# RWKV-7 then squared-Relu FFN: the state products by channel, products spread over array quarters, Relu squared in SBUF

## The chip, the cores and the metric

One core of a Trainium2 chip runs the whole program in one launch. The metric is the device time of that launch in microseconds. Thirteen runs of the kernel before gave a median of 1091.98 us (1089.86 to 1101.07).

The engines are TensorE (PE for its matmuls, PEld for its weight loads), VectorE (DVE), ScalarE (ACT), GpSimd (POOL) and SyncE (SP, which only issues transfers here). Each runs its own queue in program order and waits on semaphores for the others.

## The reference

Two blocks follow each other. The first is a recurrence over 768 tokens for 4 batches, 8 heads and 40 channels a head; the second a feed-forward network over all 3072 tokens.

```python
for t in range(S):                                   # B=4, H=8, S=768, D=40
    y[:, :, t] = einsum('bhd,bhde->bhe', rt, state)
    Sa = einsum('bhde,bhe->bhd', state, at)
    state_decay = state * wt[:, :, None, :] - einsum('bhd,bhe->bhde', Sa, bt)
    state = state_decay + einsum('bhd,bhe->bhde', vt, kt)
x = y.transpose(0, 2, 1, 3).reshape(B * S, H * D)    # 3072 x 320
h = maximum(x @ w_in, 0.0)                           # 320 x 2048
out = (h * h) @ w_out                                # 2048 x 320
```

Everything is float32.

## The kernel before

The sequence is cut into 6 chunks of 128 tokens; with 4 batches that makes 24 slots, numbered in the order chunk by chunk (`order`). Inside a chunk the recurrence is written as matrix products with a triangular inverse T, which is solved on POOL for several slots at once (`solve`), stored to DRAM and fetched back (`inverses`). Heads lie in pairs: head h is pair q = h//2, and half e = h%2 of the 128 partitions (40 of each 64 partitions are used, the rest are zero pads). The states are tiles of 128 x (4 pairs, 2 heads, 64), of which only the blocks of a head with itself are nonzero; the mask `same` keeps the others at zero.

Each slot consists of generators whose steps `weave` hands out over 12 common steps, in the order of the list `jobs`. What a generator emits in a step is appended to the queues of the engines in exactly that order; nothing is reordered afterwards.

- `chain(i)` is the serial part of slot i. It forms X = A'S + Av (tokens on partitions) from the masked product A, v, aT and the state; solves it in two halves of 64 tokens: T times the first half, N times that added to the second half, T times the second half; turns the result (`xnT`), grows the state by k'v + b'x, forms the masked product RX, and then the output y, which DVE scales into `tokens`. Between these products an ACT copy takes the result out of PSUM.
- `rest(i+1)` makes what the next slot needs: kvT (DVE, L503), the masked product A, the turned r and v (ACT copies L513 and L515), the state's decay (`f`, L521 to L524), the masked product RV, and k and b scaled.
- `prepare(i+8)` turns w, b, a, scans the decays, takes reciprocals (L357, L358, DVE), and forms N, which ACT copies out (L369) and SP stores for POOL's `solve`.
- `some(second, n)` runs n steps of the feed-forward network on groups of three finished slots: for each pair of the 16 blocks of 128 hidden channels, products of the tokens with `w_third` and `w_in`, Relu by ACT (L641), its product by DVE (L642); then the products with `w_out`.

PSUM is split into pools: `ps_w` with 4 banks (everything that `rest` and `prepare` turn or multiply, and RX), `ps_c` with 2 banks (the chain), `ps_f` with 2 banks (feed-forward). An allocation takes a bank whose last reader has been emitted, and its first product waits for that reader.

In slots 0 to 3 no feed-forward work runs; from slot 4 on ten feed-forward steps go into each slot; the last group of three slots is multiplied after slot 23, alone.

A float32 matmul shows as two records of weight load and matmul in the trace, a transposition as one.

Of the kernel before, what the change touches and what calls it, by code (L numbers as in the profile page):

```python
# [11 lines left out]
Alu = mybir.AluOpType  # L12
# [5 lines left out]
def kernel(  # L18
# [129 lines left out]
    def load(i, g=None):  # L148
        x_ = loaded[i] = {"k": fetch("k", k, i)}
        if g is not None:  # L150
# [14 lines left out]
    nc.gpsimd.memset(upper, 1.0)  # L165
    nc.gpsimd.affine_select(out=upper, in_=upper, compare_op=Alu.is_gt, fill=0.0, base=0,
                            pattern=[[1, 128]], channel_multiplier=-1)

    same = single("same", [128, NP, 2])
    nc.gpsimd.memset(same, 0.0)  # L170
    for e in range(2):
        nc.gpsimd.memset(same[e * DP:(e + 1) * DP, :, e:e + 1], 1.0)

    more_rings()
    x_ = loaded[0] = {nm: fetch(nm, src, 0) for nm, src in (("k", k), ("r", r))}
# [167 lines left out]
    def early(i, g=None):  # L343

        x_ = early_loaded.pop(i)
        dec = decays.next() if g is None else new("dec", [128, 3, NP, C + 2], 2)
        if g is not None:
            nc.vector.memset(dec[:, :A_, :, MID:MID + 1], 1.0)
        up, down, aT = (dec[:, n] for n in (UP, DOWN, A_))
        wT = turn(x_["w"])  # L350
        yield
        for q in range(NP):
            nc.vector.tensor_tensor_scan(up[:, q, MID + 1:C + 1], wT[:, q, MID:], ones, 1.0, Alu.mult, Alu.mult)  # L353
            nc.vector.tensor_tensor_scan(down[:, q, MID - 1::-1], wT[:, q, MID - 1::-1], ones, 1.0, Alu.mult, Alu.mult)
        yield
        bT_, aT_ = turn(x_["b"]), turn(x_["a"])
        nc.vector.reciprocal(down[:, :, MID + 1:C + 1], up[:, :, MID + 1:C + 1])  # L357
        nc.vector.reciprocal(up[:, :, :MID], down[:, :, :MID])  # L358
        yield
        bT = turned("bT", 1)  # L360
        nc.vector.tensor_tensor(bT, bT_, down[:, :, 1:C + 1], Alu.mult)
        nc.vector.tensor_tensor(aT[:, :, :C], aT_, up[:, :, :C], Alu.mult)  # L362
        if g is None:
            store(kept_e[i], dec)
        yield
        bb, c = order[i]
        t_ = new("N", [128, H, C], 1)
        for e, p_ in enumerate(products(bT, aT[:, :, :C])):
            nc.scalar.copy(t_[:, e * NP:(e + 1) * NP], p_)  # L369
        joins = lambda half: t_[half * HC:half * HC + Q, :, half * HC + Q:(half + 1) * HC]  # L370
        for half in range(2):
            for n in range(2):
                at = half * HC + n * Q
                if i < SMALL:
                    kept, to = kept_q[i, :, half, n], at + Q
                else:
                    u = unit_of[i]
                    kept, to = kept_d[u][i - units[u][0], :, half], (half + 1) * HC
                    kept = kept[:, n * Q * HC:n * Q * HC + Q * (to - at)].rearrange("h (s t) -> h s t", s=Q)
                store(kept.rearrange("h s t -> s h t"), t_[at:at + Q, :, at:to], 1, nc.scalar if g is not None and n else nc.sync)  # L380
            if i < SMALL and g is None:
                store(kept_m[i][half], joins(half), 1)
        if g is None:
            store(kept_n[i], t_[:HC, :, HC:], 1)
        else:
            g["dec"], g["N"] = dec, new("N21", [HC, H, HC], 2)
            nc.scalar.copy(g["N"], t_[:HC, :, HC:])
            g["joins"] = spare("joins", i)
            for half in range(2):
                nc.scalar.copy(g["joins"][half * HC:half * HC + Q], joins(half))  # L390
        yield
# [99 lines left out]
    def rest(i, g):  # L491
        bb, c = order[i]
        x_ = loaded.pop(i)
        dec = g["dec"]
        up, down, aT = dec[:, UP], dec[:, DOWN], dec[:, A_, :, :C]
        ends = new("ends", [128, NP], 2)
        g["up"], g["aT"] = up, aT
        yield

        kT, rT = turned("kvT", 1), turned("rT", 2)  # L500
        kT_ = turn(x_["k"])
        yield
        nc.vector.tensor_tensor(kT, kT_, down[:, :, 1:C + 1], Alu.mult)  # L503
        nc.vector.tensor_copy(ends, down[:, :, 0])
        joining = inverses(i, g) if i else iter(())
        if soon(i):
            next(joining, None)
        yield
        g["A"] = masked("A", 2, kT, aT)
        yield  # L510
        while "v" not in x_:
            line.pop(0)[1]()
        nc.scalar.copy(rT, turn(x_["r"]))  # L513
        vT = turned("kvT", 1)
        nc.scalar.copy(vT, turn(x_["v"]))  # L515
        g["rT"] = rT
        yield
        if c > 0:
            st = states.tiles[bb]
            f_ = new("f", [128, NP, 2], 1)  # L520
            nc.vector.tensor_tensor(f_[:, :, 0], ended[bb], ends, Alu.mult)  # L521
            nc.vector.tensor_copy(f_[:, :, 1], f_[:, :, 0])
            nc.vector.tensor_tensor(f_, f_, same, Alu.mult)
            nc.vector.tensor_tensor(st[:, :, :, :D], st[:, :, :, :D],  # L524
                                    f_.unsqueeze(3).to_broadcast([128, NP, 2, D]), Alu.mult)
        g["RV"] = masked("RV", 4, vT, rT)
        if i and unit_of[i] < FINE:
            next(joining)
        yield
        p_ = psum(ps_w)  # L530
        for q in range(NP):
            nc.tensor.transpose(p_[:, q * 128:(q + 1) * 128], down[:, q, 1:C + 1], ident)  # L532
        inv = p_.rearrange("t (h d) -> t h d", h=H)[:, :, :D]
        yield
        for nm in ("k", "b"):
            nc.vector.tensor_tensor(x_[nm][:, :, :D], inv, x_[nm][:, :, :D], Alu.mult)
            g[nm] = x_[nm]
        g["v"] = x_["v"]
        if c > 0:
            p_ = psum(ps_c)  # L540
            for q in range(NP):
                nc.tensor.transpose(p_[:, q * 128:(q + 1) * 128], st[:, q].rearrange("p e d -> p (e d)"), ident)  # L542
            sd = g["sd"] = new("sd", [128, NP, 2, DP], 2)
            nc.scalar.copy(sd.rearrange("p q e d -> p q (e d)"), quads(p_))
        yield
        yield from joining
        yield


    ended, tokens = {}, {}  # L550
    order_of = lambda h: (h % 2) * NP + h // 2

    def chain(i, g):
        bb, c = order[i]
# [1 line left out]
        aT, rT, k_, b_, v_ = (g[x] for x in ("aT", "rT", "k", "b", "v"))  # L556
        sd = g.get("sd")
        first, second_ = slice(0, HC), slice(HC, C)
        x_ = by_head(psum(ps_c))
        for h in range(H):  # L560
            mm(x_[:, h], g["A"][h % 2][:, h // 2], v_[:, h, :D], h == 0)
        if c > 0:
            for q in range(NP):
                mm(x_[:, 2 * q:2 * q + 2], aT[:, q], st[:, q, :, :D], False)
        xr = new("xr", [128, H, D], 1)
        nc.scalar.copy(xr[first], x_[first])
        yield
        T, N = g["T"], g["N"]
        xn = minus_x.next()
        xs = by_head(psum(ps_c))  # L570
        for h in range(H):
            mm(xs[first, h], T[first, order_of(h)], xr[first, h], h == 0)
        nc.scalar.copy(xn[first, :, :D], xs[first])
        yield
        for h in range(H):
            mm(x_[second_, h], N[:, order_of(h)], xn[first, h, :D], False)
        nc.scalar.copy(xr[second_], x_[second_])  # L577
        yield
        for h in range(H):
            mm(xs[second_, h], T[second_, order_of(h)], xr[second_, h], h == 0)  # L580
        nc.scalar.copy(xn[second_, :, :D], xs[second_])
        yield
        p_ = psum(ps_c)
        for q in range(NP):
# [2 lines left out]
        nc.scalar.copy(xT, quads(p_))  # L587
        yield
        if c < NCH - 1:
            grown = psum(ps_c)[:, :NP * 2 * D].rearrange("p (q e d) -> p q e d", q=NP, e=2)  # L590
            for q in range(NP):
                mm(grown[:, q], pair(k_, q), v_[:, 2 * q:2 * q + 2, :D], q == 0)
            for q in range(NP):
                mm(grown[:, q], pair(b_, q), xn[:, 2 * q:2 * q + 2, :D], False)
            nc.vector.tensor_tensor(st[:, :, :, :D], grown, st[:, :, :, :D], Alu.add)
            ended[bb] = new(f"end{bb}", [128, NP], 1)
            nc.vector.tensor_copy(ended[bb], g["up"][:, :, C])
            yield
# [27 lines left out]
    def ffn():  # L626
        for gi in range(len(order) // GB):
# [4 lines left out]
            for f in range(0, NF, 2):  # L632
# [4 lines left out]
                for e, p_ in enumerate(ps):  # L637
# [1 line left out]
                        mm(p_, w_in[:, j, (f + e) * 128:(f + e + 1) * 128], t_[:, j, :], False)  # L639
                    h_ = hidden[:, f + e]  # L640
                    nc.scalar.activation(h_, p_, Act.Relu)  # L641
                    nc.vector.tensor_tensor(h_, p_, h_, Alu.mult)  # L642
                    hid.append(h_)
                    yield True
            while left():
# [118 lines left out]
    for i in range(len(order)):  # L764
# [1 line left out]
        n, begin = share.get(i, (10, 0))  # L766
        tc.no_sync_barrier()
        g = ready.pop(i)
        jobs = [(chain(i, g), 9, 0, TOTAL) if i else (first_slot, 8, 0, TOTAL)]
        if i + 1 < len(order):  # L770
            if i:
                ready[i + 1] = {}
                load(i + 1, ready[i + 1])
            jobs.append((rest(i + 1, ready[i + 1]), 9, 2, TOTAL))
        made = ahead.get(i, ())
        for j, m_ in enumerate(made):
            jobs.append((prepare(m_), 5, j * 5, TOTAL - 5 * (len(made) - 1 - j)))
        done.update(made)
        jobs.append((some(second, n), n, begin, TOTAL))
        if i in pieces_in:  # L780
            m_, end = pieces_in[i]
            jobs.append((some(rounded, 2 * m_), 2 * m_, 0, end))
# [38 lines left out]
```

## Time and profile before

| what | value |
|---|---|
| median of 13 runs | 1091.98 us |
| the profiled execution | 1096.39 us, of which the span from first to last instruction 1094.7 us |
| PE busy | 994.3 us (91%), 7248 matmul records |
| DVE, ACT, POOL busy | 471.7 us (43%), 235.6 us (22%), 651.4 us (60%) |
| mean granted clock of TensorE | 0.906 |
| chain that ended last | PE 73%, DVE 8%, DMA 7%, POOL 7% |

In the page, a group is one line of code, engine, operation and shape: its busy time, the mean of one instruction, and the idle time before it with what ended it. A matmul's duration contains its latency, and matmuls overlap; what a group of matmuls costs PE is read from the timeline, as the start of the group after it minus its own start.

### The profile page before, as it was taken

The page shows a single profiled execution, that of the slowest core. Times are in us where ns is not written, and L with a number is a line of the kernel's source. Part 1 is how long each engine was busy: PE and PEld are TensorE (multiplying, and loading weights), DVE is VectorE, ACT ScalarE, POOL GpSimd, SP SyncE. Part 2 cuts the span into 40 slices and gives each one's busy share as a digit, 9 for nine tenths or more (in the row PEclk, how much of TensorE's full clock was granted, in tenths as well). Part 3 has the DMA queues.
Part 4 walks back from the last instruction along what each step waited for, and adds up shares of the span by engine and source line. Part 5 has one row for each costly group of instructions (what it writes and reads, how often), then busy time and mean ns, then how long its engine had stood idle before and what let it go on. Part 6 is the DMA issues. An engine that isn't in the chain of part 4 may idle for free.

```text
span 1094.7 us, 18413 instructions
## 1 busy us (share of the span) xinstructions
PE 994.3 (91%) x7248; PEld 745.9 (68%) x7248; DVE 471.7 (43%) x940; ACT 235.6 (22%) x483; POOL 651.4 (60%) x1127
## 2 busy tenths in 40 slices
PE   6386667889999999999999999999999999999798
PEld 5275556777677767777677667766786777667556
DVE  6458676687463264333462453252323322331030
ACT  2133232342221113113211222113112211230020
POOL 5787636884885999923999903999858820000000
PEclk8666655569999999999999999999999999999899
DMA  9879977749729615348616528424244331330000
GB/s 119 150 145 184 170 208 149 153 121 175 141 53 214 125 48 96 97 116 157 127 47 114 119 83 156 114 54 80 54 115 92 68 85 31 75 62 7 22 1 18
DMA packets 261350, 113.42 MB, mean 104 GB/s; under 512 B 243792, under 2 KB 249424, under 8 KB 259600
## 3 DMA queue, kind: packets, MB, share of 16 engines
q1 hardware_dynamic: 256928, 93.24, 43.1%
q0 software_dynamic: 3248, 18.88, 7.2%
q8 instruction: 57, 0.93, 0.4%
q10 hardware_dynamic: 1088, 0.13, 0.1%
q14 instruction: 29, 0.24, 0.1%
HBM read 75.77 MB, written 34.48 MB: 101 GB/s over the span
## 4 chain that ended last, share of the span: by engine, by line
PE 73%; DVE 8%; DMA 7%; POOL 7%; issue 3%; SPq 2%; ACT 1%; DVEq 0%; POOLq 0%; ACTq 0%
PE ps_f L87 34%; PE ps_c L87 19%; PE ps_w L87 13%; PE ps_w L316 4%; POOL half_t L434 3%; POOL half_p L432 3%; DMA blocks<-kept_t 1%; DVE decay L357 1%; SPq L108 1%; DMA half_n<-kept_d 1%; PE ps_w L532 1%; DVE decay L358 1%; PE ps_c L542 1%; DMA kept_e<-decay 1%; PE ps_c L585 1%
## 5 line engine op out<-in xcount | busy, mean ns | idle before, releaser
L432 POOL TENSOR_TENSOR half_p<-half_n,half_t 128x70 f32<-128x70 f32 (+52 forms) x502 | 288.9, 576 | 101.5 <-DMA half_n<-kept_d 52.2
L434 POOL TENSOR_TENSOR half_t<-half_t,half_p 128x70 f32<-128x70 f32 (+52 forms) x502 | 314.8, 627 | 39.3
L87 PE MATMUL ps_f<-w_out,hid 128*128 128x320 f32 x672 | 197.7, 438 | 0.0
L87 PE MATMUL ps_f<-tokens,w_in 128*128 128x384 f32 x448 | 171.8, 508 | 0.0
L642 DVE TENSOR_TENSOR hid<-ps_f,hid 128x384 f32<-128x384 f32 x112 | 61.7, 551 | 229.9 <-ACT hid L641 229.2
L87 PEld LDWEIGHTS ps_f<-w_out,hid 128*128 128x128 f32 x672 | 121.4, 190 | 43.7 <-issue 0.2
L87 PEld LDWEIGHTS ps_f<-tokens,w_in 128*128 128x128 f32 x448 | 77.2, 192 | 63.3 <-issue 32.2
L641 ACT ACTIVATE hid<-ps_f 128x384 f32<-128x384 f32 x112 | 54.9, 490 | 216.0 <-PE ps_f L87 216.0
L87 PEld LDWEIGHTS ps_c<-xr,T 64*64 64x64 f32 x768 | 54.4, 149 | 26.2 <-issue 21.7
L87 PE MATMUL ps_c<-xr,T 64*64 64x40 f32 x768 | 60.3, 240 | 4.4 <-ACT xr L577 1.8
L87 PE MATMUL ps_f<-tokens,w_third 64*128 64x384 f32 x224 | 62.4, 540 | 0.8 <-DVE hid L642 0.8
L87 PEld LDWEIGHTS ps_c<-in_v,A 128*128 128x128 f32 x384 | 53.2, 217 | 4.1
L87 PE MATMUL ps_c<-in_v,A 128*128 128x40 f32 x384 | 52.6, 302 | 0.0
L332 DVE TENSOR_TENSOR A<-ps_w,upper 128x512 f32<-128x512 f32 x48 | 30.9, 685 | 47.2 <-PE ps_w L87 47.2
L409 POOL DMA_DIRECT2D half_n<-kept_d x18 | 8.9, 501 | 68.4 <-DMA kept_d<-N 68.1
L332 DVE TENSOR_TENSOR RX<-ps_w,upper 128x512 f32<-128x512 f32 x48 | 30.8, 684 | 39.8 <-PE ps_w L87 39.7
L353 DVE TENSOR_TENSOR_SCAN decay<-ps_w,ones 128x64 f32<-128x64 f32 x88 | 23.5, 267 | 51.2 <-PE ps_w L316 51.2
L503 DVE TENSOR_TENSOR kvT<-ps_w,dec 128x512 f32<-128x512 f32 x24 | 16.4, 682 | 63.7 <-PE ps_w L316 36.7
L87 PE MATMUL ps_w<-decay,bT 40*128 40x128 f32 x352 | 28.3, 306 | 16.2 <-DVE decay L362 12.3
L87 PE MATMUL ps_w<-rT,xnT 40*128 40x128 f32 x384 | 33.0, 298 | 10.0 <-DVE RV L332 8.6
L87 PEld LDWEIGHTS ps_w<-rT,xnT 40*128 40x128 f32 x384 | 27.5, 199 | 20.5 <-DVE RV L332 14.5
L614 DVE TENSOR_TENSOR tokens<-ps_c,dec 128x512 f32<-128x512 f32 x24 | 16.5, 688 | 57.1 <-PE ps_c L87 57.1
(138 smaller groups left out, 1456.7 us busy)
## 6 DMA issues: line engine op xcount, KB each, us to landing
kept_e<-decay SPq DMA_DIRECT2D x22, 780.0 KB
dec<-kept_e SPq DMA_DIRECT2D x22, 780.0 KB
hid<-in_moe_w_out_dram SPq DMA_DIRECT2D x16, 320.0 KB
half_n<-kept_d POOLq DMA_DIRECT2D x12, 384.0 KB, 10.0
half_n<-kept_d POOLq DMA_DIRECT2D x6, 768.0 KB, 10.4
in_w<-in_w_dram SPq DMA_DIRECT2D x24, 160.0 KB
in_ab<-in_b_dram SPq DMA_DIRECT2D x24, 160.0 KB
in_ab<-in_a_dram SPq DMA_DIRECT2D x24, 160.0 KB
```

The costliest lines, as they stand in the source:

```text
L87: nc.tensor.matmul(o, l_, r_, start=start, stop=True, skip_group_check=True)
L108: later(lambda: queue.dma_start(out=out_, in_=in_), steps)
L316: nc.tensor.transpose(p_[:, q * 128:(q + 1) * 128], pair(x_, q), ident)
L332: nc.vector.tensor_tensor(t_, p_, over4(upper), Alu.mult)
L353: nc.vector.tensor_tensor_scan(up[:, q, MID + 1:C + 1], wT[:, q, MID:], ones, 1.0, Alu.mult, Alu.mult)
L357: nc.vector.reciprocal(down[:, :, MID + 1:C + 1], up[:, :, MID + 1:C + 1])
L432: nc.gpsimd.tensor_tensor(p_, part[:, at:at + m_].unsqueeze(1).to_broadcast([128, n, m_]), t3[:, :n, s:s + 1].to_broadcast([128, n, m_]), ...
L434: nc.gpsimd.tensor_tensor(t3[:, :n, s + 1:], t3[:, :n, s + 1:], p_, Alu.subtract)
L503: nc.vector.tensor_tensor(kT, kT_, down[:, :, 1:C + 1], Alu.mult)
L614: nc.vector.tensor_tensor(t_, y_, g["up"][:, :, :C], Alu.mult)
L641: nc.scalar.activation(h_, p_, Act.Relu)
L642: nc.vector.tensor_tensor(h_, p_, h_, Alu.mult)
```

## The change

1. In `chain`, X is formed transposed: for each head, v (128 tokens x 64) and the head's state block (64 x 64) are the stationary operands, and A and aT move past them (128 columns). Each head's result lies in its own 64 partitions, channels on partitions. ACT copies it out, four transpositions bring it back to tokens on partitions, and one ACT copy takes it into `xr`. This adds one step with a wait of PE for ACT.
2. For odd heads the two halves of 64 tokens are swapped: in X by reading A and aT in the order second half, first half; in N by where `prepare` copies N out (one ACT copy of 128x512 becomes three of 64x4x64). So in `times_t` even and odd heads use the array quarters (0,0) and (64,64) in turn, and N's products write output columns 64 to 127 and 0 to 63 in turn. Every copy out of these products becomes two of half the size.
3. The state's growth is made head by head (8 products of 64x40 from each of k and b, written to the head's 64 partitions) in place of pair by pair (4 of 128x80), and added and decayed by two DVE operations each of 64 partitions. The mask `same` and two small DVE operations on `f` go.
4. In the feed-forward network DVE squares the Relu from SBUF (`h_ * h_`) in place of multiplying it with the PSUM bank.
5. `jobs`: the feed-forward steps stand right behind the chain's, then `prepare`, then `rest`; before, it was chain, `rest`, `prepare`, feed-forward. The chain's steps are handed out as 11 (10 in slot 0) where they were 9 (8).

```diff
@@ early
-        for e, p_ in enumerate(products(bT, aT[:, :, :C])):
-            nc.scalar.copy(t_[:, e * NP:(e + 1) * NP], p_)
+        even, odd = products(bT, aT[:, :, :C])
+        nc.scalar.copy(t_[:, :NP], even)
+        for half in range(2):
+            own_, other = (slice(n * HC, (n + 1) * HC) for n in (half, 1 - half))
+            nc.scalar.copy(t_[own_, NP:, own_], odd[other, :, other])
+        nc.scalar.copy(t_[:HC, NP:, HC:], odd[:HC, :, HC:])
@@ rest
-            nc.vector.tensor_copy(f_[:, :, 1], f_[:, :, 0])
-            nc.vector.tensor_tensor(f_, f_, same, Alu.mult)
-            nc.vector.tensor_tensor(st[:, :, :, :D], st[:, :, :, :D],
-                                    f_.unsqueeze(3).to_broadcast([128, NP, 2, D]), Alu.mult)
+            for e in range(2):
+                own_ = st[e * DP:(e + 1) * DP, :, e, :D]
+                nc.vector.tensor_tensor(own_, own_, f_[e * DP:(e + 1) * DP].unsqueeze(2).to_broadcast([DP, NP, D]), Alu.mult)
@@ chain
-        for h in range(H):
-            mm(x_[:, h], g["A"][h % 2][:, h // 2], v_[:, h, :D], h == 0)
+        xw = quads(psum(ps_c))
+        for h, q, e, rows in heads:
+            mm(swap(xw[rows, q], 0), v_[:, h, :], swap(g["A"][e][:, q], e), h < 2)
         if c > 0:
-            for q in range(NP):
-                mm(x_[:, 2 * q:2 * q + 2], aT[:, q], st[:, q, :, :D], False)
+            for h, q, e, rows in heads:
+                mm(swap(xw[rows, q], 0), st[rows, q, e, :], swap(aT[rows, q], e), False)
+        xc = turned("xnT", 1)
+        nc.scalar.copy(xc, xw)
+        yield
+        p_ = psum(ps_c)
+        for q in range(NP):
+            nc.tensor.matmul(p_[:, q * 128:(q + 1) * 128], xc[:, q], ident, start=q == 0, stop=True, is_transpose=True, ...)
+        x_ = p_.rearrange("t (h d) -> t h d", h=H)[:, :, :D]
         xr = new("xr", [128, H, D], 1)
-        nc.scalar.copy(xr[first], x_[first])
+        nc.scalar.copy(xr, x_)
         yield
...
+        def times_t(half):
+            xs = psum(ps_c)[:, :NP * D].rearrange("p (q d) -> p q d", q=NP)
+            for h, q, e, _ in heads:
+                rows = halves[half ^ e]
+                mm(xs[rows, q], T[rows, order_of(h)], xr[rows, h], h < 2)
+            nc.scalar.copy(xn[halves[half], ::2, :D], xs[halves[half]])
+            nc.scalar.copy(xn[halves[half], 1::2, :D], xs[halves[1 - half]])
...
+        for h, q, e, _ in heads:
+            mm(x_[halves[1 - e], h], N[:, order_of(h)], xn[first, h, :D], False)
+        nc.scalar.copy(xr[second_, ::2], x_[second_, ::2])
+        nc.scalar.copy(xr[first, 1::2], x_[first, 1::2])
...
-            for q in range(NP):
-                mm(grown[:, q], pair(k_, q), v_[:, 2 * q:2 * q + 2, :D], q == 0)
-            for q in range(NP):
-                mm(grown[:, q], pair(b_, q), xn[:, 2 * q:2 * q + 2, :D], False)
-            nc.vector.tensor_tensor(st[:, :, :, :D], grown, st[:, :, :, :D], Alu.add)
+            for l_, r_ in ((k_, v_), (b_, xn)):
+                for h, q, e, rows in heads:
+                    mm(grown[rows, q], l_[:, h, :], r_[:, h, :D], l_ is k_ and h < 2)
+            for e in range(2):
+                rows = slice(e * DP, (e + 1) * DP)
+                nc.vector.tensor_tensor(st[rows, :, e, :D], grown[rows], st[rows, :, e, :D], Alu.add)
@@ ffn
-                    nc.vector.tensor_tensor(h_, p_, h_, Alu.mult)
+                    nc.vector.tensor_tensor(h_, h_, h_, Alu.mult)
@@ the slots
-        jobs = [(chain(i, g), 9, 0, TOTAL) if i else (first_slot, 8, 0, TOTAL)]
+        jobs = [(chain(i, g), 11, 0, TOTAL) if i else (first_slot, 10, 0, TOTAL)]
+        jobs.append((some(second, n), n, begin, TOTAL))
+        (prepare for each of ahead[i])
         if i + 1 < len(order):
             ...
             jobs.append((rest(i + 1, ready[i + 1]), 9, 2, TOTAL))
-        (prepare for each of ahead[i])
-        jobs.append((some(second, n), n, begin, TOTAL))
```

## The prediction

> **What bounds the kernel now.** I read the page's slices first, then busy time by slot, then the timeline of one slot for PE, then the waits.
>
> ```profile
> PE   6386667889999999999999999999999999999798
> PEclk8666655569999999999999999999999999999899
> ...
> 497.54:537.46 39.92, 39.24 (x289) 27.43 (x288) 19.64 (x39) 9.90 (x20) 24.20 (x38) 1.00 0.74 156
> ```
>
> From about 230 us on PE never rests, at full clock from about 312 us. The windows row is slot 10 (from its Av to the next one): of 39.92 us PE is busy 39.24, DVE 19.64, ACT 9.90. So from slot 4 to the end a microsecond taken from PE's stream is a microsecond of time, and a new wait of PE costs in full. Before 230 us PE, DVE, POOL and transfers wait for each other. The timeline of PE says what each group costs: start of the next minus own start.
>
> ```profile
> 490.24 1.09 PE L87 MATMUL ps_c<-RV,in_k 128*64 128x128 f32 x16
> 491.16 1.04 PE L87 MATMUL ps_c<-RX,in_b 128*64 128x128 f32 x16
> ...
> 497.54 1.87 PE L87 MATMUL ps_c<-in_v,A 128*128 128x40 f32 x16
> 499.24 1.10 PE L87 MATMUL ps_c<-state,dec 128*128 128x80 f32 x8
> 500.27 0.92 PE L87 MATMUL ps_f<-tokens,w_third 64*128 64x384 f32 x4
> ...
> 502.60 1.12 PE L87 MATMUL ps_c<-xr,T 64*64 64x40 f32 x16
> 503.66 0.66 PE L316 MATMUL ps_w<-ident,in_w 128*128 128x128 f32 x4
> ...
> 514.49 0.60 PE L585 MATMUL ps_c<-ident,minus_x 128*128 128x128 f32 x4
> 515.02 1.16 PE L87 MATMUL ps_w<-dec,kvT 40*128 40x128 f32 x16
> 516.11 1.12 PE L87 MATMUL ps_c<-in_v,in_k 128*128 128x80 f32 x8
> 517.07 1.06 PE L87 MATMUL ps_c<-minus_x,in_b 128*128 128x80 f32 x8
> 517.96 0.60 PE L316 MATMUL ps_w<-ident,in_r 128*128 128x128 f32 x4
> ```
>
> Av costs 1.70 us, 106 ns a record, though only 40 columns move: loading 128 weight columns sets it. The form 128*64 with 128 columns moving, even and odd heads on the two column halves, costs 0.92 us for 16 (57 ns).
>
> **Part 1, X by channel.** Av takes just that form: 1.70 to 0.92, -0.78. A'S: 8 records in 1.03 become 16 of 64*64 with 128 columns, on opposite quarters; the A product (40*128, alternating row halves) costs 1.09 for 16, so 1.0 is taken: 0. One more change of form between the two: +0.10. Four transpositions as at 514.49: +0.53. Sum -0.15. Their waits for ACT (0.59 for 128x512, 0.42 for `xr`) lie behind a feed-forward step of 1.4 to 2.3 us.
>
> **Part 2, quarters.** T costs 1.06 for 16, 66 ns, again loading weights. With neighbours on opposite quarters two can load at once; what then? The smallest records of the trace:
>
> ```profile
> 194.75 1.09 PE L87 MATMUL ps_w<-blocks,hid 32*32 32x32 f32 x32
> 195.77 2.61 PE L87 MATMUL ps_c<-in_v,A 128*128 128x40 f32 x15
> ```
>
> 1.02 us for 32, 32 ns each. So 16 x 32 plus 0.10 for the change of form: 0.61, -0.45 each; T twice and N (1.06 too): -1.35. Bounds: 0 if they don't overlap, -0.53 at half.
>
> Two rules of the Trainium skill speak against this. "TensorE: Matmul & The Clock Gate", Part 2, puts PE's sequencer at about 62 ns per matmul where hardware decoding is off; then T at 66 is at the floor already and part 2 brings nothing. The 32 ns above decides against it. "TensorEngine Tiling", Restrictions and Gotchas (PSUM Pressure), says that different row tiles can't access one PSUM bank at once. T's quarters and A'S are different row tiles in one bank; the trace's row-tiled products (A, RV) write two banks, so no full group tests it. By the rule T stays at 1.06 twice and A'S goes to 16 x 112 ns = 1.8 us (112 as the 128-column records of the state's product run now): +1.7 a slot against my sum. In the 32x32 group, halves on different row tiles share a bank, and no gap shows inside it; their partitions differ, as here. I take the overlap.
>
> **Part 3, growth.** 0.96 + 0.89 = 1.85 becomes 32 records of 128*64 with 40 columns. RV's 57 ns is for 128 columns moving; if loads on the two column halves overlap, 32 x 32 + 0.10 = 1.1, -0.75; if not, 32 x 58 = 1.86 and nothing. I take the first: in the RV group the loads start in pairs 7 ns apart. DVE: two operations more and two fewer (0.17 to 0.57 each), hidden.
>
> PE in a slot: -0.15 - 1.35 - 0.75 = -2.25 with growth (15 slots, 5 to 19), -1.5 without (20 to 23), about -2.0 in slot 4: -33.8 - 6.0 - 2.0 = **-42 us**.
>
> **Part 5, the order: what now waits.** In step 5 of a slot the feed-forward step stands before kvT on DVE, and A comes one step later with only the turn of xn between. In the slot above:
>
> ```profile
> 514.69 0.49 ACT L641 ACTIVATE hid<-ps_f 128x384 f32<-128x384 f32 x1 [2.22 <-PE ps_f L87]
> 515.21 0.56 DVE L642 TENSOR_TENSOR hid<-ps_f,hid 128x384 f32<-128x384 f32 x1 [2.34 <-ACT hid L641]
> ...
> 518.60 0.59 ACT L513 COPY rT<-ps_w 128x512 f32<-128x512 f32 x1 [2.83 <-PE ps_w L316]
> 519.08 0.59 ACT L515 COPY kvT<-ps_w 128x512 f32<-128x512 f32 x1
> ```
>
> kvT (0.68) would run after 515.77, end at 516.4, and A start at 516.45 in place of 515.02: 1.43 us. It happens where step 5 is a hidden block (slots 7, 8, 10, 13, 15, 16, 18, 19, 21, 22); where it is a `w_out` step DVE has nothing before kvT. With part 4's wait below 1.6: **+16**. Then r and v are turned directly before RX, which takes their two banks: v's copy ends at 519.67, and RX, free to start at 518.83 by PE, starts at 519.7 less two records: 0.85 in slots 4 to 19, **+13.6**. RV then waits for RX's masks behind the reciprocals (3.4 us on DVE): the wait for RX covers nearly all, **+2**.
>
> What goes: the waits before the turn of the decays and before RX.
>
> ```profile
> PE ps_w L87 <- DVE RV L332: 8.6, 5, 3.1
> PE ps_w L532 <- DVE RX L332: 8.3, 12, 1.2
> ```
>
> RX, y and a feed-forward step now lie between: **-15** of these 16.9. Net of the order: +17.
>
> **Part 4, the square from SBUF.** The bank is free 0.56 us sooner, but PE waited for `hid` under 1 us in all (L642 delays PE by 0.8): 0. What it costs:
>
> ```profile
> L523 DVE TENSOR_TENSOR f<-f,same x20: 166/168/1099, 222.9 to 985.8; 128x8 f32<-128x8 f32 x20
> ```
>
> An operation with two SBUF inputs takes 168 ns, or up to 1099 where POOL is at work (570 at 523.30); L642, reading PSUM, never leaves 487 to 559. So the square will wait up to a POOL instruction, some 0.3 us in the mean, which counts only where PE waits for DVE (in the 1.6). POOL waits too: some 17 squares of 0.3 us per solve of 131 us, +5; T of slots 10, 14 and 18 lands some 20 us before its use, the slots' gain takes 6: hidden.
>
> ACT gains about 1.7 us a slot (copies halved, X's copy, N's three) on 9.90 of 39.92: hidden. In slots 0 to 4 nothing covers the new step (PE waits 0.6 to 0.9 for each copy, N's copies 0.6 later for POOL), while PE's saving counts double at the half clock. Between +4 and -8; I take -2. SP's and POOL's transfers keep their order within their slots; `same`'s memsets (under 1 us) are in this.
>
> **Sum:** 1096.39 - 42 + 17 - 2 = 1069.4 on the profiled execution, which lay 4.4 above the median: 1065 for the median.
>
> **Rivals.**
> A, the forecast: 1065, own range 1050 to 1078 (waits for A and RX half or double by 7, early slots -8 to +4). Chance 0.60.
> B, column halves don't overlap their loads: N and growth bring nothing, 15 x 1.2 + 4 x 0.45 + 1 = +21: 1086. For it: no group in the trace is bound by loads on alternating columns. 0.14.
> C, the bank rule holds: T and A'S lose 1.7 a slot in 19 slots, +32: 1097, slower. It decides from 1.4 a slot on, where PE's remaining saving no longer pays for the +17. Against it: the 32x32 group, and that the quarters' partitions differ. 0.13.
> D, the new waits are mostly covered (DVE's kvT or ACT's copies come early): +17 becomes 0: 1048. Against it: the queues are in order. 0.08.
> E, POOL and DVE hold each other up so that T arrives late in slots 10, 14 and 18, some 4 us each, and the waits double: about 1098. 0.05.
> That the products don't alternate as the change says: in the program's order they take quarters (0,0) and (64,64) in turn, so no.
>
> **Numbers.** About 0.3% (3.3 us) is what a measurement can tell. Faster: A, D and most of B: 0.77. Same: part of B and C: 0.06. Slower: C and E: 0.17. The range leaves out E's upper half, part of C and D's lower part: 1046 to 1096.
>
> **What would show it.** T's group near 0.6 us, N's the same, growth near 1.1, Av near 0.95; PE idle before A released by DVE kvT in hidden-block slots, before RX by ACT kvT in all of 4 to 19, and none before the turn of the decays; a slot of some 38.5 us for 39.9. Wrong if T stays at 1.06 or A'S at 1.8 (C), growth at 1.85 (B), or if slots 0 to 4 move by over 8 us.

## The result and the profile after

The changed kernel takes 1060.04 us (median of 11 runs, 1055.22 to 1068.03), the kernel before 1092.84 us (median of 48): ratio 0.9705, interval 0.9685 to 0.9725. That is 32.8 us less. The prediction was 1065, 27 us less on its own profiled execution; the profiled execution of the changed kernel took 1062.1 us, 34.3 less than the one it was predicted from.

First the page of the changed kernel: the slices of PE and its clock, and the row of the square.

```profile
PE   6375668769999999999999999999999999999898
...
PEclk8666556578889999999999999998999999999899
...
L664 DVE TENSOR_TENSOR hid<-hid 128x384 f32<-128x384 f32 x128 | 95.1, 743 | 244.2 <-ACT hid L663 243.9
```

PE is full from the same slice on as before. The clock row has an 8 in the middle where before had only 9s. The square from SBUF takes 743 ns in the mean; the product that read PSUM took 551 before.

Then slot 10, which is the slot that the prediction showed. The windows row gives span, PE, PEld, DVE, ACT, POOL, then the granted clock and DMA:

```profile
481.42:520.61 39.19, 37.61 (x318) 25.27 (x316) 20.36 (x40) 11.40 (x26) 21.28 (x34) 0.96 0.66 131
```

39.19 us for 39.92 is a poor slot: PE is idle for 1.6 us of it and the clock stands at 0.96 in place of 1.00. Both show in PE's timeline of the slot. What a group costs is the next start minus its own:

```profile
481.42 1.09 PE L87 MATMUL ps_c<-A,in_v 128*64 128x128 f32 x16
482.45 1.10 PE L87 MATMUL ps_c<-dec,state 64*64 64x128 f32 x16
483.48 0.92 PE L87 MATMUL ps_f<-tokens,w_third 64*128 64x384 f32 x4
...
485.71 0.60 PE L577 MATMUL ps_c<-ident,xnT 128*128 128x128 f32 x4
486.15 1.46 PE L87 MATMUL ps_f<-tokens,w_in 128*128 128x384 f32 x4
...
487.97 0.66 PE L87 MATMUL ps_c<-xr,T 64*64 64x40 f32 x16
488.56 0.92 PE L87 MATMUL ps_f<-tokens,w_third 64*128 64x384 f32 x4
...
490.90 0.66 PE L87 MATMUL ps_c<-minus_x,N 64*64 64x40 f32 x16
491.49 1.56 PE L87 MATMUL ps_f<-tokens,w_in 128*128 128x384 f32 x4
...
496.25 0.60 PE L606 MATMUL ps_c<-ident,minus_x 128*128 128x128 f32 x4
498.18 1.16 PE L87 MATMUL ps_w<-dec,kvT 40*128 40x128 f32 x16 [1.34 <-DVE kvT L503]
499.27 0.67 PE L87 MATMUL ps_c<-in_v,in_k 128*64 128x40 f32 x16
499.76 0.77 PE L87 MATMUL ps_c<-minus_x,in_b 128*64 128x40 f32 x16
500.46 2.93 PE L87 MATMUL ps_f<-tokens,w_in 128*128 128x384 f32 x4
...
504.68 0.60 PE L311 MATMUL ps_w<-ident,in_v 128*128 128x128 f32 x4
505.51 1.53 PE L87 MATMUL ps_w<-rT,xnT 40*128 40x128 f32 x15 [0.24 <-ACT rT L513]
```

Av costs 1.03 us for 1.70, A'S 1.03, the turn of X 0.44, T and N 0.59 each for 1.05. Growth is 1.19 here (499.27 to 500.46) and 1.06 in 13 of 20 slots, for 1.85. Before A stands the new wait: 496.25 to 498.18, of which 1.34 us is named as idle. DVE shows why, the square first and kvT behind it:

```profile
496.97 0.56 DVE L664 TENSOR_TENSOR hid<-hid 128x384 f32<-128x384 f32 x1 [1.34 <-ACT hid L663]
497.44 0.68 DVE L503 TENSOR_TENSOR kvT<-ps_w,dec 128x512 f32<-128x512 f32 x1
```

Just behind that wait the feed-forward group at 500.46 costs 2.73 us where 1.4 is usual. The windows of 2 us there say that this is the clock (the trace's own clock records put it at 0.50 from 500.13 to 503.54 us):

```profile
500.00:502.00 2.00, 2.00 (x17) 1.32 (x14) 1.40 (x5) 0.00 (x0) 1.41 (x5) 0.53 0.94 113
502.00:504.00 2.00, 2.00 (x9) 1.29 (x8) 0.04 (x1) 0.49 (x1) 1.69 (x5) 0.61 0.96 151
```

To see where the whole gain lies I added up PE's timelines of both traces over slots 5 to 19, where the stream is dense. A group is charged from its start to the next start; where the last record of a group and the first of the next start over 0.7 us apart, that counts as a wait, less 0.2. The 15 slots took 608.7 us before and 587.3 after.

| term, slots 5 to 19, us | predicted | measured |
|---|---|---|
| Av, A'S, turn of X | -2.3 | -9.4 + 1.4 + 6.6 = -1.5 |
| T and N | -20.3 | -13.8 - 6.9 = -20.7 |
| growth | -11.3 | -9.4 |
| wait before A | +13 (8 slots by 1.6) | +13.5 |
| wait for the decays at the same place, slot 5 | - | +2.1 |
| wait for ACT before RX | +12.8 | +5.2 |
| waits of before that go | -15 | -11.5 |
| products with `w_third` | 0 | -6.8 |
| two short waits of before (T, `w_in`) | - | -1.9 |
| RV behind RX's masks | +2 | in the rest |
| rest (5.1 of it half clock) | - | +9.6 |
| sum | -21 | -21.4 |

Slots 0 to 4 gave 6.4 us and slots 20 to 23 with the end 6.9; the prediction had 4 and about 3 there.

### The profile page after: what moved, and what is told of

Read it like the earlier page. It is cut to its first block, busy times and chain, and to the rows that moved or that the text cites. A ratio compares the mean times of both kernels' runs of the same rounds, so it can differ in the third digit from the quotient of the medians.

```text
span 1060.4 us, 19794 instructions
## 1 busy us (share of the span) xinstructions
PE 946.7 (89%) x7824; PEld 685.6 (65%) x7824; DVE 501.6 (47%) x940; ACT 272.0 (26%) x627; POOL 667.2 (63%) x1124
## 4 chain that ended last, share of the span: by engine, by line
PE 77%; DVE 6%; DMA 6%; issue 3%; ACT 3%; POOL 3%; SPq 1%; DVEq 0%; POOLq 0%; ACTq 0%
PE ps_f L87 38%; PE ps_c L87 17%; PE ps_w L87 16%; PE ps_w L311 4%; POOL half_t L434 1%; POOL half_p L432 1%; DMA in_w<-in_w_dram 1%; DMA dec<-kept_e 1%; SPq L108 1%; DMA in_k<-in_k_dram 1%; DMA kept_e<-decay 1%; DVE decay L352 1%; PE ps_c L577 1%; DMA w_out<-in_moe_w_in_dram 1%; PE ps_w L531 1%
## 5 line engine op out<-in xcount | busy, mean ns | idle before, releaser
L434 POOL TENSOR_TENSOR half_t<-half_t,half_p 128x70 f32<-128x70 f32 (+52 forms) x502 | 323.3, 644 | 39.4
L664 DVE TENSOR_TENSOR hid<-hid 128x384 f32<-128x384 f32 x128 | 95.1, 743 | 244.2 <-ACT hid L663 243.9
L87 PE MATMUL ps_f<-tokens,w_in 128*128 128x384 f32 x448 | 179.9, 526 | 0.0
L87 PEld LDWEIGHTS ps_w<-decay,bT 40*128 40x128 f32 x352 | 25.1, 213 | 37.3 <-DVE decay L357 21.4
L87 PE MATMUL ps_w<-dec,kvT 40*128 40x128 f32 x384 | 33.0, 318 | 16.4 <-DVE kvT L503 16.4
L327 DVE TENSOR_TENSOR RX<-ps_w,upper 128x512 f32<-128x512 f32 x48 | 30.8, 682 | 32.8 <-PE ps_w L87 32.5
L87 PEld LDWEIGHTS ps_w<-dec,kvT 40*128 40x128 f32 x384 | 27.9, 217 | 21.7 <-DVE kvT L503 19.2
L87 PEld LDWEIGHTS ps_w<-rT,kvT 40*128 40x128 f32 x384 | 28.8, 210 | 15.7 <-DVE RX L327 7.2
L327 DVE TENSOR_TENSOR RV<-ps_w,upper 128x512 f32<-128x512 f32 x48 | 30.9, 685 | 16.3 <-PE ps_w L87 15.9
L87 PE MATMUL ps_w<-rT,kvT 40*128 40x128 f32 x384 | 34.3, 310 | 4.6 <-DVE RX L327 3.5
L352 DVE RECIPROCAL decay<-decay 128x256 f32<-128x256 f32 x22 | 38.3, 1739 | 0.0
## 6 DMA issues: line engine op xcount, KB each, us to landing
half_n<-kept_d POOLq DMA_DIRECT2D x6, 768.0 KB, 10.4
```

The costliest lines, as they stand in the source:

```text
L87: nc.tensor.matmul(o, l_, r_, start=start, stop=True, skip_group_check=True)
L327: nc.vector.tensor_tensor(t_, p_, over4(upper), Alu.mult)
L434: nc.gpsimd.tensor_tensor(t3[:, :n, s + 1:], t3[:, :n, s + 1:], p_, Alu.subtract)
L664: nc.vector.tensor_tensor(h_, h_, h_, Alu.mult)
```

## The experiments

Each undoes or moves one thing in the changed kernel. Ratios are to the kernel before; the changed kernel stands at 0.9705, and "beside after" means against its 1060.04 us.

**e1: the same products, even heads first, then odd.** Neighbours in program order then lie on one array quarter (T, N) or one column half (growth).

```diff
+    in_rows = sorted(heads, key=lambda x: x[2])
-            for h, q, e, _ in heads:          # times_t, N, growth
+            for h, q, e, _ in in_rows:
```

> The changed kernel, with the heads of T, N and the growth taken in the order 0, 2, 4, 6, 1, 3, 5, 7, so that neighbours stay on the same quarter or column half; instructions and data are otherwise the same. Theory (two small products gain by loading side by side on different quarters): T and N go back to about 1.05 us a group, growth to about 1.9, PE pays 2.1 us more in 15 slots and 1.35 in 4, and the ratio to the kernel before is about 1.00 (1.060 ms + 37 us). Rival (the gain lies in the copies, the order, or the smaller moving size): T stays near 0.6 and the ratio near 0.97.

Measured: 0.9901 (0.9866 to 0.9936), 1078.57 us, 18.5 beside after: between the theory (1.00) and the rival (0.97), and half of the some 37 us that were expected. Its timeline of PE says that the groups did not go back to their old costs:

```profile
578.14 0.92 PE L87 MATMUL ps_c<-xr,T 64*64 64x40 f32 x16
578.99 2.42 PE L87 MATMUL ps_f<-w_out,hid 128*128 128x320 f32 x8
...
582.87 0.74 PE L87 MATMUL ps_c<-in_v,in_k 128*64 128x40 f32 x13
583.39 0.25 PE L87 MATMUL ps_c<-minus_x,in_b 128*64 128x40 f32 x1
583.44 0.23 PE L87 MATMUL ps_c<-in_v,in_k 128*64 128x40 f32 x1
...
583.58 0.72 PE L87 MATMUL ps_c<-minus_x,in_b 128*64 128x40 f32 x13
584.23 2.42 PE L87 MATMUL ps_f<-w_out,hid 128*128 128x320 f32 x8
```

T costs 0.85 us, between 0.59 (alternating) and 1.05 (one quarter), growth 1.36 between 1.06 and 1.85. In the single records of T the first five starts, of even heads, lie 58 to 79 ns apart; then a record starts only 6 ns after the one before it. A record of `minus_x,in_b` starts at 583.39, while one of `in_v,in_k`, which stands ahead of it in the program, starts at 583.44. So PE reaches ahead for a product of the other quarter or half, and the grouped order only delays the overlap. The gain is the overlap of quarters and halves, and the order of the heads decides how much of it is had. In e1's profiled execution, which at 1072.7 us lay below its median, T, N and growth cost 16.2 us more over slots 5 to 19 than after. These slots are only 8.3 us longer, among other things because 17.2 us of them ran at half clock, and 28.6 after.

**e2: the old order of `jobs`.** Chain, `rest`, `prepare`, feed-forward, with all else as changed.

```diff
-        jobs.append((some(second, n), n, begin, TOTAL))
-        (prepare for each of ahead[i])
         ...
             jobs.append((rest(i + 1, ready[i + 1]), 9, 2, TOTAL))
+        (prepare for each of ahead[i])
+        jobs.append((some(second, n), n, begin, TOTAL))
```

> The changed kernel with the old order of the jobs (chain, rest, prepare, feed-forward); the chain keeps its 11 steps. Theory: no wait for kvT before A any more (-16 us), none for the copies of r and v before RX (-8), but RX and RV now stand next to each other, so RV waits for RX's masks, 1.3 us and more behind the reciprocals in 16 slots (+21 to +35): ratio 0.965 to 0.985. Rival (the new order is what brought the gain, the products little): ratio 0.99 or more.

Measured: 0.9633 (0.9621 to 0.9645), 1052.36 us: the new order costs 7.7 us beside the old one, where the prediction had 17. The 13.5 us before A are gone. In their place RV waits for DVE's mask of RX, 11.1 us over slots 5 to 19 and not the 21 to 35 expected, and in slot 10 PE waits once for r:

```profile
500.00 1.11 PE L311 MATMUL ps_w<-ident,in_r 128*128 128x128 f32 x4 [4.80 <-DMA in_r<-in_r_dram]
...
505.29 1.16 PE L87 MATMUL ps_w<-rT,xnT 40*128 40x128 f32 x16
507.27 1.64 PE L87 MATMUL ps_w<-rT,kvT 40*128 40x128 f32 x15 [0.81 <-DVE RX L327]
```

By slots, the old order gains 12.4 us in slots 4 and 5 (50.41 to 44.55, 46.13 to 39.55) and 10.2 in slots 16 to 19, where `prepare` no longer runs; it loses 5.2 in slots 2 and 3, and 12.9 in slots 6 to 15. Neither order is the better one everywhere.

**e3: the square from PSUM again.**

```diff
-                    nc.vector.tensor_tensor(h_, h_, h_, Alu.mult)
+                    nc.vector.tensor_tensor(h_, p_, h_, Alu.mult)
```

> The changed kernel with Relu times the PSUM bank again in place of the square from SBUF. Theory: the square from SBUF cost waits of DVE for POOL (mean 743 ns against 557) and lengthened POOL's work; undone, L664's mean is 557 again, the wait before A shorter in slots where POOL works (2.1 to 2.5 us go to 1.6), and the time is 2 to 5 us less: ratio 0.966 to 0.969. Rival (the bank that comes free sooner saves PE waits): PE waits before w_third come back, and the time is more: ratio over 0.972.

Measured: 0.9775 (0.9749 to 0.9801), 1068.65 us, 8.6 slower beside after. Here the theory fell, and the rival's ratio came out: part 4 is worth something. In the profiled executions slots 5 to 19 are 5.9 us longer than after. The wait before A is 2.2 us smaller in e3 (11.3 for 13.5 over slots 5 to 19; the square takes 557 ns and no longer meets POOL), but the products with `w_third` cost 8.2 more (47.3 for 39.1). First e3, PE and DVE, then the changed kernel at the same place of the slot:

```profile
520.82 1.72 PE L87 MATMUL ps_f<-tokens,w_third 64*128 64x384 f32 x4
522.47 1.56 PE L87 MATMUL ps_f<-tokens,w_in 128*128 128x384 f32 x4
...
521.02 0.56 DVE L664 TENSOR_TENSOR hid<-ps_f,hid 128x384 f32<-128x384 f32 x1 [1.31 <-ACT hid L663]
```

```profile
515.25 1.12 PE L87 MATMUL ps_f<-tokens,w_third 64*128 64x384 f32 x4
516.30 1.56 PE L87 MATMUL ps_f<-tokens,w_in 128*128 128x384 f32 x4
```

1.65 us for four records against 1.05. In the single records the starts lie 427, 380 and 427 ns apart in e3, and 214 apart after. The record lengths (587, 482, 587, 483 ns in e3; 587, 587, 482, 483 after) show that the records of the two blocks come one block after the other in e3 and in turn after, where both banks of `ps_f` are free. In e3 the third record starts at 521.63, right after the square, which reads the second bank, has ended (521.02 and 0.56 are 521.58). With the square in SBUF that bank is free when Relu ends. PE's rows name no wait here: the time is inside the group, and not a wait before it as the rival had it.

**e4: kvT one step earlier.** The one `yield` that stands before kvT's product in `rest` goes behind it, so kvT is on DVE before the feed-forward step's square.

```diff
         kT_ = turn(x_["k"])
-        yield
         nc.vector.tensor_tensor(kT, kT_, down[:, :, 1:C + 1], Alu.mult)
         nc.vector.tensor_copy(ends, down[:, :, 0])
+        yield
```

> The changed kernel with the product kvT given to DVE one step earlier, in the step in which k is turned, so that it stands ahead of that step 5's square. Theory: the wait before A (202 ns without, 1610 and more with it, in 11 slots) goes, 16 us less: ratio about 0.956. Rival (another wait takes its place, DVE standing still for k's turn or for the decays' transfer): less than 6 us, ratio over 0.965.

Measured: 0.9603 (0.9585 to 0.9622), 1049.77 us, 10.3 faster beside after. In slot 10 the turn of xn goes straight over into A:

```profile
496.39 0.60 PE L606 MATMUL ps_c<-ident,minus_x 128*128 128x128 f32 x4
496.92 1.16 PE L87 MATMUL ps_w<-dec,kvT 40*128 40x128 f32 x16
```

The wait is gone in all ten slots, so the step named for it is shown. Slots 5 to 19 are 12.2 us shorter. The halved clock behind those waits goes too: half-clock time in these slots falls from 28.6 to 18.8 us, and of the four stretches behind a wait before A none is left. Against that slot 5 takes 2.6 us more, and in slot 18 T comes 3.8 us late. The whole lies between the theory (16) and the rival (under 6).

**e5: growth by pair again**, with `same` and the two small operations on `f` as they were.

```diff
-            for l_, r_ in ((k_, v_), (b_, xn)):
-                for h, q, e, rows in heads:
-                    mm(grown[rows, q], l_[:, h, :], r_[:, h, :D], l_ is k_ and h < 2)
+            for q in range(NP):
+                mm(grown[:, q], pair(k_, q), v_[:, 2 * q:2 * q + 2, :D], q == 0)
+            for q in range(NP):
+                mm(grown[:, q], pair(b_, q), xn[:, 2 * q:2 * q + 2, :D], False)
```

> The changed kernel with the growth pair by pair again (and with it the mask and the four operations of the decay). Theory: the growth costs 1.85 us for 1.16, 0.69 more in 15 slots and some in slots 0 to 4, 10 to 14 us in all: ratio 0.980 to 0.984. Rival (the growth's saving was given back by its smaller DVE operations or by waits behind it): under 4 us, ratio below 0.974.

Measured: 0.9928 (0.9903 to 0.9953), 1083.02 us: 23.0 us beside after, more than theory (10 to 14) and rival (under 4) had. Growth in two of its slots, once at full clock and once behind a wait:

```profile
389.07 1.12 PE L87 MATMUL ps_c<-in_v,in_k 128*128 128x80 f32 x8
390.03 1.06 PE L87 MATMUL ps_c<-minus_x,in_b 128*128 128x80 f32 x8
390.92 1.50 PE L87 MATMUL ps_f<-tokens,w_in 128*128 128x384 f32 x4
...
428.53 1.84 PE L87 MATMUL ps_c<-in_v,in_k 128*128 128x80 f32 x8
430.17 1.91 PE L87 MATMUL ps_c<-minus_x,in_b 128*128 128x80 f32 x8
431.88 2.85 PE L87 MATMUL ps_f<-tokens,w_in 128*128 128x384 f32 x4
```

1.85 us and 3.35. Over its 20 slots growth takes 47.9 us in e5, 25.9 after and 42.0 before. The difference of 22.0 holds 20 times 0.79 = 15.8 at full clock, where the theory took 0.69 in 15 slots. The other 6.2 fall where the clock is halved (11.6 us lost in growth's groups for 5.4 after): in slots 1 to 3, in slot 5, and behind the waits before A in slots 8, 13, 15 and 18. Growth comes right behind A, so it stands in the halved stretch and costs double there.

**e6: X by tokens and no quarters** (parts 1 and 2 undone: Av and A'S as before, N unswapped, T and N on one quarter; growth, square and order as changed).

```diff
-            mm(swap(xw[rows, q], 0), v_[:, h, :], swap(g["A"][e][:, q], e), h < 2)
+            mm(x_[:, h], g["A"][h % 2][:, h // 2], v_[:, h, :D], h == 0)
...
-                mm(xs[rows, q], T[rows, order_of(h)], xr[rows, h], h < 2)
...
-        even, odd = products(bT, aT[:, :, :C])
+        for e, p_ in enumerate(products(bT, aT[:, :, :C])):
+            nc.scalar.copy(t_[:, e * NP:(e + 1) * NP], p_)
```

> The changed kernel without its parts 1 and 2: X by tokens in one step, T and N on one quarter each as before the change; growth by head, the square from SBUF and the new order stay. Theory (measured groups: Av and A'S 2.69 for 2.05, four transpositions 0.44 less, T, T and N 1.05 for 0.59 each): 1.6 us more in 19 slots, 30 us: ratio 0.995 to 1.000. Rival (the earlier gain of some 12 us in slots 2 and 3 and that behind slot 19 is due to the shorter chain, or X's step costs a wait that now goes): ratio 1.005 or more, or under 0.990.

Measured: 0.9899 (0.9866 to 0.9932), 1079.58 us, 19.5 beside after and not the 30 of the theory. T and N are back at 1.05 us, Av at 1.8. In its profiled execution, 8 us above its median, these make +33 over slots 5 to 19, and the turn of X that goes makes -6.6. The rest of the difference is the waits: with one step less in the chain they fall elsewhere, 10.4 us before A (behind growth now) and 9.0 before the turn of the decays in place of the 15.6 behind the turn of xn, while the wait before RX (4.5 at v's turn) goes:

```profile
517.58 0.64 PE L87 MATMUL ps_c<-minus_x,in_b 128*64 128x40 f32 x16
518.93 1.16 PE L87 MATMUL ps_w<-dec,kvT 40*128 40x128 f32 x16 [0.71 <-DVE kvT L498]
...
533.33 0.66 PE L526 MATMUL ps_w<-ident,dec 128*128 128x128 f32 x4 [1.40 <-DVE RV L327]
```

**e7: e4, and `rest` ahead of `prepare`** in `jobs`, which puts the copies of r and v earlier against RX.

```diff
-        (prepare for each of ahead[i])
         ...
             jobs.append((rest(i + 1, ready[i + 1]), 9, 2, TOTAL))
+        (prepare for each of ahead[i])
```

> The changed kernel with kvT one step earlier and rest ahead of prepare in each step, so that b and a are turned between v and RX. Theory: beside the wait before A, the one before RX goes in slots 6 to 15 (0.3 us at its start and about as much inside the group), 3 to 6 us: ratio 0.955 to 0.958. Rival (the masks of RX then come later behind the reciprocals and RV waits): no gain over kvT alone, 0.960 or more.

Measured: 0.9617 (0.9588 to 0.9646), 1049.33 us: nothing beside e4's 1049.77, as the rival had it. In slots 5 to 19 the wait for ACT before RX falls by some 8 us against e4 (the groups of v's turn 7.5 for 11.3, of RX 15.7 for 19.8), but 4.2 us for a transfer of r in slot 10, 1.5 more for T and 3.3 before RV come in, and slots 0 to 4 take 255.2 us for 249.5.

**e8: e4, and an order by slot.** The changed order in slots 0 to 3, the old one in slots 4 and 5, feed-forward, `rest`, `prepare` from slot 6 on.

```diff
+        jobs += rests + prepares + network if i in (B, B + 1) else network + prepares + rests if i < B else network + rests + prepares
```

> As the one before, but slots 0 to 3 in the changed kernel's order and slots 4 and 5 in the old order (chain, rest, prepare, feed-forward). Theory: with the feed-forward steps early, slots 4 and 5 wait for the weights' rounding on DVE and for its PSUM banks (50.4 and 46.1 us for 44.6 and 39.5 in the run of the old order); 8 to 12 us less: ratio 0.944 to 0.950. Rival (these two slots are set by what the slots before left undone, transfers and POOL): less than 3 us, 0.953 or more.

Measured: 0.9552 (0.9521 to 0.9582), 1042.86 us. This version beats both kernels, 17.2 us below the changed one. Against e7, slots 4 and 5 are 9.5 us shorter, as the theory had it (8 to 12). The ratio still lies on the rival's side (0.953 or more) and not in the 0.944 to 0.950 expected, because PE now waits 12.7 us for T (5.1 in e7), 7.7 of them in slot 10. There POOL issues the store of T, SP the load, and PE waits for it:

```profile
473.50 0.60 POOL L437 DMA_DIRECT2D kept_t<-half_t  x1 [0.30 <-POOL half_t L434]
...
477.71 1.35 SPq L448 DMA_DIRECT2D T<-kept_t  x2
...
481.50 1.08 PE L87 MATMUL ps_c<-xr,T 64*64 64x40 f32 x16 [7.71 <-DMA T<-kept_t]
```

Before, that store was issued at 472.1 and slot 10 first used T at 502.6; after, at 471.7 and 488.0. In e8 PE is ready for T at 473.8 (481.50 less 7.71), with the store at 473.5: POOL has hardly moved and PE has come up to it. In this slot `solve` is the next limit. It is rival E's lateness of T, which the changed kernel itself does not yet have.

The other 4.98 us, in slot 18, are not POOL's. T is stored 19 us before its use, but the load stands in SP's queue behind eight moves of `tokens`. SP took 14.6 us to issue them, 7.9 of which it waited for an earlier one of them to land:

```profile
767.66 0.60 POOL L437 DMA_DIRECT2D kept_t<-half_t  x1 [0.30 <-POOL half_t L434]
767.72 14.55 SPq L108 DMA_DIRECT2D tokens<-tokens  x8
...
782.88 1.37 SPq L448 DMA_DIRECT2D T<-kept_t  x2
...
786.46 1.08 PE L87 MATMUL ps_c<-xr,T 64*64 64x40 f32 x16 [4.98 <-DMA T<-kept_t]
```

The same moves stand ahead of e4's late T in slot 18 (13.0 us, load at 786.8). In the changed kernel they took 7.1 us, with 0.4 of waiting, and the load at 795.1 was in time for the use at 801.1. In e8 POOL fetches its next `half_n` from 768.4 us on, and that lands at 781.3, just before SP goes on at 781.5; that the two transfers hold each other up is likely, not shown.

## Why the prediction was right, and where it was not

**Parts 1 to 3 came out as worked, in the cost of their groups.** Av 1.03 for 0.92 plus 0.10, the turn 0.44 for 0.53, T and N 0.59 for 0.61, growth 1.06 for 1.10. Rival B (column halves don't overlap their loads) would have left growth at 1.85: it is out. Rival C rested on the rule of "TensorEngine Tiling" on row tiles in one bank: A'S stands at 1.03, not 1.8, so in these groups two row tiles write one bank without loss. The 62 ns a matmul that "TensorE: Matmul & The Clock Gate", Part 2, gives for hardware decoding off would have held T at 1.05; T's 16 records take 37 ns each, growth's 32 records 33. The step that was right here was to take the trace's smallest records (32 ns) against the rules. What a part is worth in the whole is another number. Undone alone, parts 1 and 2 are worth 19.5 us (e6; some 30 predicted), part 3 23.0 (e5; some 12), part 4 8.6 (e3; 0), and part 5 costs 7.7 (e2; 17). These come to 43.4 and not to 32.8, since each part also moves waits and the clock.

**The wait before A was right in place and size**: ten slots, those that the prediction listed, 16.3 us beyond the usual 0.2 for the 16 predicted (13.5 of them in slots 5 to 19), and e4 removes it. Rival D (the wait is covered) is out. The square's wait for POOL is seen too: A's wait is 1.6 us in every such slot of e3, and up to 2.5 after.

**The wait before RX was sized too large.** The step took 0.85 a slot in all of 4 to 19. The turn of v to RX takes 0.51 for 0.20 us where `prepare` runs and nothing more from slot 16 on; with the slower start of RX's group it is 5.2 us over slots 5 to 19, not 12.8. RX's first records start once rT is there, which the row at 505.51 names, a copy earlier than the step had it. The prediction's sign, a wait for the copy of v in all of slots 4 to 19, did not show.

**The waits that go were sized too large as well**: -15 taken, -11.5 found in slots 5 to 19. The row `DVE RV` of 8.6 us was read as steady work, but 5.4 of it lies before 277 us, in slots where other waits take its place. A row of the waits view should be split by time before it is booked.

**Part 4 at 0 was the step that failed**: it is worth 8.6 us by the medians of e3 and after. In slots 5 to 19 of the traces `w_third`'s groups cost 8.2 less with it, and the wait before A 2.2 more. The prediction counted waits of PE that had a row, and the row was 0.8 us. The wait stands inside groups of four records, and it could only be seen in that group's own cost (1.03 us in the median of slots 5 to 19 before, 0.85 after).

**The early slots** gave 6.4 us where 4 were taken (2, and slot 4's products). Two larger shifts hide in that. Slots 2 and 3 became 12.4 us shorter: over slots 0 to 4, waits before the turn of k fell from 13.6 us to 4.3. Slot 4 took 4.8 more, 2.8 of it a wait of the first feed-forward products for DVE's rounding of `w_out`; e2 and e8, with the old order there, get the 5 us back. Why k arrives in time now was not tested.

**What was not foreseen is the half clock.** By the traces' clock records slots 5 to 19 have 28.6 us at 0.50 after and 10.2 before; half of that is lost, so the changed kernel pays 9.2 us more. Of these 5.1 stand in the +9.6 of the table's rest, 2.6 in growth's row and 1.7 in that of Av and A'S, which would otherwise have read -12.0 and -3.2. Four stretches lie at a wait before A: 3.4 us each from 500.1, 616.2 and 698.1, and 6.8 from 735.6, where A itself costs 2.01 us for 1.09. Another 6.8 us lie at the wait for the decays in slot 5. The trace of before had one such stretch too, 3.4 us from 401.5, behind waits of 0.93 us for RV and 0.58 for RX; the prediction's "full clock from about 312 us" passed over it. The other 4.5 us of the rest were not followed; RV's groups hold 2.3 of them (2 predicted), those of y's product with the state 1.6.

**The sum.** That slots 5 to 19 came out at -21.4 for -21 is luck. Too much was booked for RX (-7.6) and too little for part 4 (-6.8) and the two short waits (-1.9). Against these stood the rest (+7.6 beside RV's 2), waits booked as gone (+3.5), the decays in slot 5 (+2.1) and growth (+1.9). The early and late slots gave 6 us more than taken. So the profiled execution gained 34.3 us for the 27 predicted, and the medians came within 5 us.

## What to carry to other kernels

Compare group starts, not durations: in these traces a float32 record with 40 columns moving costs 106 ns with 128 stationary columns and 66 with 64 on one quarter, and 33 to 37 when neighbours alternate between array quarters or column halves. With 128 columns moving, alternating records still cost 57 (RV) to 64 ns (A'S). When PE is the bound, a step put ahead of another on a side engine (the square ahead of kvT) is a wait of PE: look for who needs the later one first, and move that one up by a step, as e4 did. Such a wait can cost more than its length, since the clock may halve behind it. Look for bank waits inside groups too, and ask which engine or queue becomes late once the slots get shorter.

## What the runs showed of the hardware that was not expected

- PE starts products ahead of program order where they lie on another quarter or column half (e1: 583.39 before 583.44, starts 6 ns apart after five at 58 to 79). "TensorE: Matmul & The Clock Gate", Part 3, has matmuls start strictly in order; these records do not. For PE the program order named ahead of the prediction is thus not strict.
- Short waits can halve the clock, in four of the ten places before A in this execution. The clock changes only on a grid: the halvings at 500.13, 616.18, 698.10 and 735.65 us lie 34, 58 and 69 steps of 3.413 us behind the first. In the step before each, PE was busy for 0.61, 0.61, 0.65 and 0.41 of the time. "TensorE: Matmul & The Clock Gate", Part 1, names an idle window of about 3.4 us; the step has that length, but it need not be idle.
- Idle time alone does not decide: in slot 7 PE was busy for only 0.46 of the step from 377.3 us, and the clock stayed. The work in the step tells the places apart better. Count for each record the columns moved times its share of the array (rows times columns, over 128 x 128). In all ten traces, from 300 us to slot 23, the 34 steps at full clock that a halving follows hold 0 to 1664 such columns; the other 1864 have a median of 3182, and only 18 of them hold 1664 or less. So a wait seems to count when it falls into one step together with the small products of the state. This is a sorting of records; no run tested it, and between 1232 and 1664 it leaves both outcomes.
- The square reading twice from SBUF took 743 ns in the mean: 833 in the 86 cases that overlap an instruction of POOL, 558 in the other 42. The form with one PSUM input took 557 in either case (e3). "SBUF — State Buffer", "Who interferes with whom", says that two SBUF inputs contend with POOL's reads, and the trace agrees. POOL's busy time was 650.4 us in e3 and 667.2 after. T's store in slot 10 was not later for it (471.7 for 472.1 before), so POOL's share stayed hidden; DVE's is the 2.2 us in the waits before A.
